# Bias of the third and fourth block by identity matmuls instead of vector adds, with a new written order

## The chip, the cores and the metric

The kernel runs on one core of a Trainium2 chip. A core has a matrix engine (TensorE, PE in the profile, with its weight loads listed apart as PEld), a vector engine (VectorE, DVE), a scalar engine for functions such as exp and ln (ScalarE, ACT), a general engine (GpSimd, POOL) and a queue engine that issues transfers (SyncE, SP). Each works through its own list of instructions in order, and waits are made with semaphores. Matmuls write to PSUM, eight banks of 512 f32 values in each of 128 partitions; everything else lives in SBUF. The metric is the time of one execution in microseconds (us); lower is better.

## The reference

Windowed attention with a linear distance bias and a few global keys, and after it a two-layer network with softplus, on every token:

```python
scores = scale * np.matmul(q, k.transpose(0, 1, 3, 2))      # B, H, S, D = 4, 8, 768, 64
rel = pos[:, None] - pos[None, :]
is_global = pos[None, :] < n_global                          # 8
is_local = (rel >= 0) & (rel < n_local)                      # 96
dist = np.where(is_global & ~is_local, float(n_local), np.abs(rel))
scores = scores + (-slopes[:, None, None] * dist)[None]
scores = np.where(is_global | is_local, scores, -1e9)
a = np.exp(scores - np.max(scores, axis=-1, keepdims=True))
a = a / (np.sum(a, axis=-1, keepdims=True) + 1e-09)
x = np.matmul(a, v)                                          # to 3072 tokens of 512
h = x @ w_in                                                 # 512 -> 2048
g = np.maximum(h, 0.0) + np.log1p(np.exp(-np.abs(h)))
return g @ w_out                                             # 2048 -> 512
```

## The kernel before, in words

A query block is 128 tokens of one sequence, and there are 24, numbered in the order of `UNITS` (L148): a unit is two neighbouring blocks whose q, k and v are loaded together. Blocks 0 and 1 are the first two of sequence 0, blocks 2 and 3 the first two of sequence 1. Two blocks make a group of 256 tokens for the network, 12 groups in all. With a window of 96, a block looks at its own 128 keys and, unless it is the first of its sequence, at those of the block before, into which the eight global keys are copied (`gk`, `gv`). A first block thus has 4 score tiles of 128 columns for each half of the heads (a "part"), any other has 8.

The steps of a block: q and k are cast to bf16 (`castq`, `castk`) and transposed, in units 0 to 2 by TensorE (`trq`, `trk`, L740, evacuated by `cpq`, `cpk`), from unit 3 on by transposing DMAs on the SP queue (L763, L770). The scores (`sc`, L875; L822 for block 0) go to PSUM, `s_ps[0]` and `s_ps[1]` of two banks each. The bias, a bf16 table that also holds the mask, is added in one of two ways. In `soften` (L887) VectorE adds it while it moves the scores from PSUM to an SBUF tile `z` (L901, steps `z`), and the exp on ScalarE (L908, steps `ex`) reads `z`. For blocks named in `PE_BIAS` (L157) the step `sb` (L856, and L812 for block 0) first multiplies the table by the identity matrix into the same PSUM columns, the score matmuls accumulate on it (`start=not biased`, L878), and the exp reads PSUM. No maximum is subtracted. Then come the products with v (`pv`, L927), which bring the sum of the weights in a 65th column, the division (`nm`, L938 and L939) and the transposition of the result into XT (`xt` by TensorE and `xc` in groups 0 to 2, later by DMA).

The network: `a{g}.{p}` is the first layer of group g, piece p of 8 (eight matmuls, L985, into `h_ps[p % 2]`), `e` and `ln` the softplus on ScalarE (L1000, L1011), `b` the second layer (L1032 in groups 0 and 1; from group 2 on seven products of a Strassen scheme, L519, with sums `ka` of the activations, L449, and `ws` of the weights, L414), `oe` and `oc` the evacuation and `st` the store (L557, L1064). The f32 weights arrive in eight pieces each (`win`, `wout`, L623) and are cast (`cin`, `cout`, L627). `a{g}.{p}` needs both pieces of its pair, so `a0.0` and `a0.1` need `cin0` and `cin1`, and `a0.6` and `a0.7` need `cin6` and `cin7`.

What runs where and in which order is written out in full in the string `ORDER` (L68 to L146): each word is a step and its engine (P PE, V DVE, A ACT, G POOL, S SP), and every engine works through its steps in that order. Nothing is scheduled at run time. 35 matmuls on zeros (`fill`, L1145) stand where TensorE has nothing to do in the first microseconds. Steps on SP are issued in order too, each after what it waits for; k and q of unit i are `ldk{i}.0`, `ldk{i}.1` and so on in units 0 to 2, single loads later.

Of the kernel before, what the change touches and what calls it, by code (L numbers as in the profile page):

```python
# [1300 lines left out]
```

## Time and profile before

| | |
|---|---|
| median of 3 runs | 212.99 us (211.81 to 213.7) |
| the profiled execution: time | 212.39 us |
| the profiled execution: span from first to last instruction | 210.6 us |
| mean granted TensorE clock | 0.999 |
| adds of the bias on DVE, 1024 columns (L901, biasA) | 38, mean 1216 ns |
| exp on ACT of 1024 columns from z (L908) | 38, mean 1051 ns |
| fillers on PE (L1145) | 35 |
| PE waiting for a k transposition by DMA | 1.3 us, once |
| moved by DMA | 40.98 MB |

A row of a timeline gives the start in us from the beginning of the span, how long it took, the engine and the line, the operation, what it writes and reads, and how many instructions are merged into it; in brackets stands the idle time of the engine before it and what ended that. A queue has a q behind its engine (SPq, ACTq). A matmul's record is longer than the time that it keeps PE, because matmuls overlap in the pipeline; the distance between two starts is the better measure.

### The profile page before, as it was taken

How to read it: one execution, taken by the hardware profiler on the slowest of the kernel's cores; microseconds unless marked ns; L12 is line 12 of the kernel's file. 1: busy time of each engine (PE TensorE's matmuls, PEld its weight loads, DVE VectorE, ACT ScalarE, POOL GpSimd, SP SyncE). 2: the span in 40 equal slices, each digit the busy share in tenths (PEclk: the TensorE clock that was granted, in tenths of full speed). 3: DMA queues.
4: the chain of work that ended last, by engine and by line, in shares of the span. 5: the costliest groups of instructions: out<-in, count | busy, mean ns of one | idle time of the engine just before them, and what ended most of it. 6: DMA issues, size and time to landing. Idle time of an engine off the chain costs nothing.

```text
span 210.6 us, 5494 instructions
## 1 busy us (share of the span) xinstructions
PE 201.3 (96%) x2211; PEld 164.4 (78%) x2211; DVE 156.1 (74%) x287; ACT 174.6 (83%) x248; POOL 105.5 (50%) x113
## 2 busy tenths in 40 slices
PE   5898899999999979999999999999999999999993
PEld 2465687655778868888988988888899889888883
DVE  5779699988788965889888878858883976023494
ACT  5768799998999998978789999896997999775710
POOL 4347668745954763455415783502126849129040
PEclk9999999999999999999999999999999999999999
DMA  5999999999999999999999599955641103400205
GB/s 196 337 355 386 387 357 363 336 209 242 221 304 191 221 214 271 240 166 288 209 170 225 180 181 272 146 124 128 153 99 28 25 5 102 150 0 0 103 0 199
DMA packets 70136, 40.98 MB, mean 195 GB/s; under 512 B 30432, under 2 KB 61664, under 8 KB 70112
## 3 DMA queue, kind: packets, MB, share of 16 engines
q1 hardware_dynamic: 69680, 39.99, 76.2%
q10 hardware_dynamic: 432, 0.66, 0.9%
q8 instruction: 17, 0.28, 0.6%
q14 instruction: 7, 0.06, 0.1%
HBM read 27.26 MB, written 6.29 MB: 159 GB/s over the span
## 4 chain that ended last, share of the span: by engine, by line
PE 68%; DMA 13%; POOL 5%; ACT 5%; DVE 4%; issue 2%; ACTq 0%; SPq 0%; POOLq 0%; DVEq 0%
PE h_ps L985 31%; PE o_ps L519 20%; DMA raw<-in_k_dram 5%; PE s_ps L875 4%; PE x_ps L927 4%; PE s_ps L1032 3%; DMA kT<-kb 3%; DMA raw<-in_q_dram 3%; DMA qT<-qb 2%; PE o_ps L1032 2%; POOL raw L449 2%; ACT pb L908 2%; ACT e L1000 2%; ACT g L1011 1%; POOL g L449 1%
## 5 line engine op out<-in xcount | busy, mean ns | idle before, releaser
L985 PE MATMUL h_ps<-XT,w_in_bf 128*128 128x256 bf16 x768 | 95.5, 273 | 1.5 <-POOL w_in_bf L627 1.3
L985 PEld LDWEIGHTS <-w_in_bf 128*128 128x128 bf16 x768 | 72.4, 98 | 13.1 <-POOL w_in_bf L627 1.9
L1000 ACT ACTIVATE e<-h_ps 128x512 f32<-128x512 f32 x96 | 60.2, 636 | 14.3 <-PE h_ps L985 13.9
L1011 ACT ACTIVATE g<-e 128x1024 bf16<-128x1024 f32 x48 | 50.0, 1057 | 0.4
L901 DVE TENSOR_TENSOR z<-s_ps,biasA 128x1024 f32<-128x1024 f32 x38 | 45.8, 1216 | 3.4 <-PE s_ps L875 2.0
L908 ACT ACTIVATE pb<-z 128x1024 bf16<-128x1024 f32 (+1 forms) x44 | 43.2, 992 | 1.1 <-DVE z L901 1.0
L519 PEld LDWEIGHTS <-g 128*128 128x128 bf16 x320 | 30.8, 98 | 3.6
L449 POOL TENSOR_TENSOR raw<-g 128x1024 bf16<-128x1024 bf16 x11 | 23.5, 2142 | 19.3 <-ACT g L1011 12.8
L677 POOL CAST vb<-raw 64x512 bf16<-64x512 f32 x31 | 20.4, 660 | 11.0 <-DMA raw<-in_v_dram 9.1
L449 POOL TENSOR_TENSOR g<-g 128x1024 bf16<-128x1024 bf16 x9 | 19.5, 2171 | 12.3 <-DVE raw L449 9.7
L793 POOL COPY vb<-vb 4x512 bf16<-4x512 bf16 x16 | 9.8, 612 | 31.7 <-PE x_ps L927 30.6
L519 PEld LDWEIGHTS <-raw 128*128 128x128 bf16 x240 | 23.1, 98 | 2.9
L519 PE MATMUL o_ps<-raw,raw 128*128 128x256 bf16 x192 | 24.1, 273 | 0.0
L519 PE MATMUL o_ps<-raw,g 128*128 128x256 bf16 x160 | 20.1, 273 | 0.0
L927 PEld LDWEIGHTS <-pb 128*128 128x128 bf16 x352 | 16.4, 98 | 4.3 <-ACT pb L908 0.9
L939 DVE TENSOR_TENSOR xs<-x_ps,rcp 128x256 bf16<-128x256 f32 x40 | 17.0, 424 | 1.4
L449 DVE TENSOR_TENSOR raw<-g 128x1024 bf16<-128x1024 bf16 x19 | 15.6, 827 | 2.7 <-ACT g L1011 2.7
L519 PE MATMUL o_ps<-w_out_bf,g 128*128 128x256 bf16 x128 | 16.1, 272 | 0.0
L927 PE MATMUL x_ps<-vb,pb 128*128 128x65 bf16 x304 | 15.8, 193 | 0.0
L938 DVE RECIPROCAL rcp<-x_ps 128x4 f32<-128x4 f32 x40 | 7.1, 179 | 10.3 <-PE x_ps L927 10.1
L1145 PE MATMUL x_ps<-blank 128*128 128x512 bf16 x35 | 12.2, 436 | 2.2 <-DVE blank L1084 2.2
L483 DVE TENSOR_TENSOR osb<-osb,o_ps 128x512 f32<-128x512 f32 x8 | 5.5, 686 | 10.3 <-PE o_ps L519 8.1
(109 smaller groups left out, 227.6 us busy)
## 6 DMA issues: line engine op xcount, KB each, us to landing
raw<-in_v_dram SPq DMA_DIRECT2D x12, 512.0 KB, 6.3
out_dram<-osb SPq DMA_DIRECT2D x22, 256.0 KB, 2.5
raw<-in_q_dram SPq DMA_DIRECT2D x9, 512.0 KB, 5.3
raw<-in_k_dram SPq DMA_DIRECT2D x9, 512.0 KB, 5.1
raw<-in_moe_w_in_dram SPq DMA_DIRECT2D x8, 512.0 KB, 9.3
raw<-in_moe_w_out_dram SPq DMA_DIRECT2D x8, 512.0 KB, 9.4
raw<-in_k_dram SPq DMA_DIRECT2D x6, 256.0 KB, 6.6
raw<-in_q_dram SPq DMA_DIRECT2D x4, 256.0 KB, 7.5
```

What stands on the lines that cost most here:

```text
L449: (nc.vector if eng == "DVE" else nc.gpsimd).tensor_tensor(dst, a[0], b[0], ALU.subtract)
L519: nc.tensor.matmul(psum(j), lhs[:, f // 2, f % 2, :], w(f), start=(f == 0 and not (chain and j in "267")), stop=(f == 7), skip_group_check ...
L677: copy_on[eng](dst, src)
L901: nc.vector.tensor_tensor(z, src, bias, ALU.add)
L908: nc.scalar.activation(pb[:, 0:nr, :].rearrange("p (y a) b -> p y (a b)", y=2), src, AF.Exp, scale=1.0 / root_d)
L927: nc.tensor.matmul(xv[:, h, :], pb[:, 4 * (h % 2) + 2 * part + h // 2 if lone else u_all * (2 * (h % 2) + h // 2) + u, :], vb_of(prev if u ...
L939: nc.vector.tensor_tensor(xs[:, 4 * part : 4 * part + 4, :], xv[:, :, 0:D], rcp[:][:, :, None].to_broadcast([P, 4, D]), ALU.mult,)
L985: last = nc.tensor.matmul(hv[:, j, :], w_in_bf[:, m, fb * P : fb * P + P], XT[g % NXG][:, m, :], start=(m == 0), stop=(m == NM - 1),)
L1000: nc.scalar.activation(e[:, p % 2, :, :].rearrange("p j (b t r) -> p (j b) r t", b=2, r=2), hb[:].rearrange("p (a r t) -> p a r t", a=4, r=2),
L1011: nc.scalar.activation(gt[:, 2 * p - 2 : 2 * p + 2, :].rearrange("p a t -> p (a t)"), e[:].rearrange("p a j t -> p (a j t)"), AF.Ln, bias=1.0,
L1032: nc.tensor.matmul(bank(key)[:, 0 : z - a], gt[:, fb, ns * P : ns * P + P], w_out_bf[:, fb, a:z], start=(fb == 0), stop=(fb == NFB - 1),)
L1145: nc.tensor.matmul(x_ps[:], blank[:, 0:P], blank[:])
```

## The change

`PE_BIAS` names blocks 2 and 3 as well. The four VectorE adds `z2.0`, `z2.1`, `z3.0` and `z3.1` are no longer made, and their exps read PSUM. Three steps come on TensorE: `sb2.0`, four identity matmuls of 256 columns, and `sb3.0` and `sb3.1`, two of 512 columns each. The string `ORDER` is another one throughout: steps stand elsewhere in their engine's list, and some casts, copies and sums of two operands have another engine. The loads of the first three units and of w_in are the same ones in another sequence. Everything else in the file is unchanged. Of `ORDER`, its beginning and the part around the transpositions of units 5 and 6 are shown:

```diff
 ORDER = """
-ldq0.1:A iota:G ldk0.1:S ldq0.0:A ldk0.0:S dl1a:V blank:V table:A ldq1.0:S dl1c:V fill0:P dl0a:V ldv0:S dl0b:V
-fill1:P dl0c:V ldq1.1:S fill2:P dl1e:V d0:G ident:G fill3:P ldk1.0:S biasTrue2:A d0e:V fill4:P ones:G fill5:P
-biasFalse2:V fill6:P biasFalse7:A biasFalse5:G biasFalse1:V castk0.1:A fill7:P biasFalse6:V biasTrue0:A fill8:P
-biasFalse3:A win0:S castk0.0:V biasTrue4:A fill9:P castq0.1:A castq0.0:V ldk1.1:S trk0.0:P biasTrue7:V castq1.0:A
-win1:S biasFalse0:V biasFalse4:A trq0.0:P ldv1:S cpk0.0:V fill10:P ldk2.0:S sb0.0:P cpq0.0:A biasTrue3:V fill11:P
-castv0.00:G win3:S cpk0.1:V cpq0.1:A fill12:P fill13:P biasTrue1:A fill14:P biasTrue6:G biasTrue5:V sc0.0:P fill15:P
-sb1.0:P castv0.11:G ex0.0:A win2:S castv0.01:V fill16:P ex0.1:A sc1.0:P castv0.10:G ldk2.1:S castq1.1:V sb1.1:P
-ex1.0:A pv0.0:P sc1.1:P nm0.0:V fill17:P ldq2.0:S ex1.1:A castk1.0:V pv0.1:P fill18:P castk1.1:V ldq2.1:S trq1.0:P
-nm0.1:V fill19:P trk1.0:P cpq1.1:V fill20:P cin1:G win5:S pv1.0:P cpk1.0:A cpq1.0:V pv1.1:P fill21:P cpk1.1:A
-fill22:P nm1.0:V xt0:P nm1.1:V sc2.0:P fill23:P castv1.11:A castv1.01:G win4:S fill24:P z2.1:V fill25:P xt1:P
-gv4.0:A castv1.10:G fill26:P win7:S z2.0:V fill27:P sc3.1:P xc1:A xc0:V cin0:G sc3.0:P ex2.0:A fill28:P z3.0:V
-ex2.1:A win6:S castv1.00:G a0.1:P cin3:A castk2.0:G z3.1:V wout0:S pv2.0:P a0.0:P cin2:G e0.1:A wout1:S fill29:P
-nm2.0:V a0.3:P e0.0:A castq2.0:G ldv2:S castk2.1:V ln0.0:A castq2.1:G wout3:S fill30:P pv2.1:P nm2.1:V gk4:G ex3.0:A
-trq2.0:P trk2.0:P cin5:G wout2:S cpq2.1:V xt2:P e0.3:A fill31:P a0.2:P cpk2.0:V xc2:A gv4.1:G wout4:S cin4:V
-fill32:P fill33:P e0.2:A pv3.0:P cpk2.1:V a0.5:P ex3.1:A cin7:G wout5:S nm3.0:V a0.4:P cpq2.0:V e0.5:A ln0.1:A
-pv3.1:P cin6:V sc4.0:P gv8.1:G nm3.1:V a0.7:P ldq3:S e0.4:A z4.0:V ln0.2:A cout0:G wout6:S xt3:P a0.6:P xc3:V e0.7:A
...
-z8.1:V xt7:S castv4.01:G a2.7:P e2.4:A castv4.11:V b1.1.12:P ex8.1:A ldq6:S ws3.1:V pv8.0:P a2.6:P st0.1.0:S ln2.2:A
-nm8.0:V trq5:S gk9:G b1.1.14:P castv4.10:V e2.6:A pv8.1:P sc9.0:P e2.7:A nm8.1:V gv9.1:G trk5.0:S castv5.00:A a3.0:P
-oc1.1.0:V castv5.11:G ln2.3:A ws3.7:G z9.0:V a3.1:P st1.1.0:S xt8:S e3.0:A b2.3:P ka2.7:V ex9.0:A a3.2:P gv9.0:V
-st0.0.0:S ka2.5:G z9.1:V e3.1:A ldv6:S b2.4:P ldk6:S e3.2:A ka2.1:V trk5.1:S ex9.1:A pv9.0:P a3.3:P castv5.10:G
-gk10:A a3.4:P ln3.0:A nm9.0:V ka2.6:V pv9.1:P e3.3:A sc10.0:P nm9.1:V gv10.0:G oe2.a:A a3.5:P e3.4:A z10.1:V ka2.2:G
-xt9:S b2.1:P e3.5:A ex10.1:A a3.6:P ldq7:S oe2.1:V ldv7:S gv10.1:G a3.7:P ln3.1:A z10.0:V gk11:G castv6.11:G b2.5:P
-e3.6:A castq6.0:V ex10.0:A castk6.0:G sc11.0:P trq6:S a4.0:P e3.7:A z11.0:V ln3.3:A castv5.01:G a4.1:P trk6.0:S
-castv6.01:G e4.0:A b2.2:P ex11.0:A trk6.1:S pv10.0:P a4.2:P oe2.c:V castq7.0:A nm10.0:V b2.7:P ldk7:S e4.1:A z11.1:V
-ldv8:S pv10.1:P ln3.2:A b2.6:P gv11.0:G nm10.1:V e4.2:A a4.3:P ka3.1:V ex11.1:A gv11.1:V a4.4:P oe2.7:V e4.3:A
-pv11.0:P ka3.7:V st2.1.0:S b3.3:P ln4.0:A xt10:S nm11.0:V ka3.5:G sc12.0:P ln4.1:A pv11.1:P b3.4:P z12.1:V trq7:S
...
+blank:V table:A ones:G ldk0.0:S ldq0.0:A iota:G fill0:P ldk0.1:S ldq0.1:A fill1:P ident:G dl1a:V fill2:P ldv0:S
+fill3:P ldq1.0:S dl0a:V dl0b:V fill4:P dl1c:V fill5:P dl0c:V dl1e:V fill6:P d0:G biasTrue1:A ldk1.0:S d0e:V fill7:P
+biasTrue0:A biasFalse1:V fill8:P castk0.0:G biasFalse2:A ldq1.1:S biasTrue7:V fill9:P biasFalse7:A fill10:P
+biasFalse6:A fill11:P biasTrue6:A ldk1.1:S castq0.0:V fill12:P fill13:P biasFalse5:V castk0.1:G win1:S biasTrue4:V
+castq0.1:A biasTrue3:A trk0.0:P ldv1:S biasFalse0:V biasTrue5:V biasFalse4:A trq0.0:P biasTrue2:A cpk0.1:V
+biasFalse3:A fill14:P fill15:P cpq0.1:A fill16:P cpk0.0:V fill17:P win0:S cpq0.0:A sb0.0:P castv0.01:V castv0.10:G
+sc0.0:P castv0.11:V fill18:P sb1.0:P ex0.0:A castv0.00:G sc1.0:P ex0.1:A castq1.0:V sb1.1:P ex1.0:A sc1.1:P ldq2.1:S
+castk1.0:V pv0.0:P fill19:P win2:S castk1.1:G fill20:P nm0.0:V ex1.1:A fill21:P win3:S fill22:P castq1.1:G ldk2.0:S
+trq1.0:P ldk2.1:S pv0.1:P trk1.0:P cpq1.0:A ldq2.0:S nm0.1:V pv1.1:P fill23:P cpk1.0:A cpq1.1:V pv1.0:P fill24:P
+cpk1.1:A castv1.00:G win4:S xt0:P nm1.0:V fill25:P cin1:G sb2.0:P xc0:V sc2.0:P nm1.1:V win5:S castv1.01:G fill26:P
+cin0:V fill27:P ex2.0:A xt1:P win7:S fill28:P gv4.1:G castv1.10:A fill29:P sb3.0:P xc1:V ex2.1:A sc3.0:P castq2.1:G
+pv2.0:P a0.0:P gv4.0:A win6:S nm2.0:V castv1.11:G ex3.0:A fill30:P pv2.1:P cin2:G a0.1:P wout0:S e0.0:A nm2.1:V
+wout1:S castk2.0:V sb3.1:P cin3:G e0.1:A wout3:S fill31:P sc3.1:P fill32:P xt2:P castk2.1:G ex3.1:A a0.2:P xc2:V
+castq2.0:G ln0.0:A pv3.0:P cin4:V ldv2:S a0.3:P nm3.0:V e0.2:A trk2.0:P gk4:V e0.3:A pv3.1:P cin5:V trq2.0:P
+cpk2.1:A nm3.1:V a0.5:P cpq2.0:A cpk2.0:V cin7:G ln0.1:A a0.4:P cpq2.1:V wout2:S e0.5:A xt3:P cin6:V sc4.0:P e0.4:A
+wout6:S ln0.2:A gk8:V a0.7:P z4.1:V ws0.6:G a0.6:P e0.7:A xc3:V ex4.1:A fill33:P cout1:V fill34:P a1.1:P ldq3:S
...
+b1.1.14:P ex8.0:A st0.0.0:S a2.7:P ldq6:S ws3.4:V castv4.00:G a2.6:P trk5.1:S ex8.1:A castv4.01:V e2.7:A oc1.1.0:V
+pv8.0:P gk9:G st1.0.0:S castq5.0:G e2.6:A sc9.0:P nm8.0:V ln2.2:A a3.1:P z9.1:V ws3.3:G trq5:S ln2.3:A a3.0:P z9.0:V
+castv4.11:G pv8.1:P trk5.0:S b2.3:P e3.0:A gv9.0:G e3.1:A nm8.1:V a3.2:P castv4.10:G ex9.0:A ka2.7:V ldk6:S gv9.1:G
+a3.3:P xt8:S e3.2:A ka2.6:V ex9.1:A b2.4:P castv5.00:G ka2.1:V ldv6:S pv9.0:P e3.3:A a3.4:P castv5.01:G gk10:A
+oe2.a:A nm9.0:V a3.5:P ln3.1:A castq6.0:V pv9.1:P ka2.5:V e3.4:A sc10.0:P ldv7:S gv10.0:G nm9.1:V ln3.0:A b2.1:P
+gv10.1:G z10.1:V xt9:S e3.5:A a3.6:P ka2.2:G oe2.1:V ex10.1:A a3.7:P ldq7:S z10.0:V e3.6:A b2.5:P gk11:A e3.7:A
+castv6.00:V trq6:S castk6.0:G sc11.0:P ex10.0:A b2.2:P z11.0:V castv6.11:G ln3.2:A st1.1.0:S pv10.0:P trk6.0:S
+a4.0:P castv6.01:G nm10.0:V castv7.10:G a4.1:P oe2.c:V e4.0:A trk6.1:S castv5.11:G z11.1:V pv10.1:P a4.2:P e4.1:A
+gv11.1:G ldv8:S ex11.0:A gv11.0:V castv7.01:G b2.7:P castv6.10:V ln3.3:A b2.6:P nm10.1:V e4.2:A castq7.0:V a4.3:P
+ln4.0:A oe2.7:V a4.4:P ka3.7:V ex11.1:A sc12.0:P ka3.1:V ka3.5:G ldq8:S pv11.0:P e4.3:A b3.3:P z12.0:V xt10:S
...
 BIASA_ON = ["ACT"]
-PE_BIAS = (0, 1)
+PE_BIAS = (0, 1, 2, 3)
 PE_KEYS = {
```

More of the change, by code (lines that the diff above doesn't have):

```diff
@@ new lines @@
+sc6.0:P oc1.0.0:A nm5.1:V castv3.01:A gv6.1:G ldk5:S z6.0:V xt5:P castv3.00:G b1.1.0:P xc5:A b1.1.2:P gv6.0:G z6.1:V
+b1.1.4:P ex6.0:A a2.1:P castk4.0:G trq4:S ex6.1:A pv6.0:P a2.0:P ws2.7:G nm6.0:V gk7:A e2.1:A trk4.0:S pv6.1:P
+sc7.0:P e2.0:A nm6.1:V castv5.10:G a2.3:P ln2.0:A z7.0:V gv7.0:G ldq5:S a2.2:P gv7.1:G trk4.1:S z7.1:V ex7.0:A
+castv3.10:G b1.1.6:P b1.1.8:P ldv4:S ws1.6:V ex7.1:A pv7.0:P b1.1.10:P nm7.0:V st0.1.0:S ws3.1:G sc8.0:P e2.3:A
+pv7.1:P xt6:S e2.2:A a2.5:P nm7.1:V ln2.1:A ws3.7:G z8.0:V a2.4:P xt7:S e2.5:A castk5.0:G b1.1.12:P z8.1:V e2.4:A
@@ new lines @@
+ln4.1:A nm11.0:V b3.4:P z12.1:V ldk7:S pv11.1:P a4.5:P oe3.a:A nm11.1:V ka3.6:G ex12.1:A sc13.0:P xt11:S e4.4:A
+b3.1:P ex12.0:A z13.0:V e4.5:A pv12.0:P trq7:S a4.6:P castq8.0:G nm12.0:V ex13.0:A a4.7:P oe3.1:V ldk8:S e4.6:A
+ka3.2:V pv12.1:P b3.5:P castk7.0:G e4.7:A z13.1:V castv7.00:A st2.1.0:S b3.2:P ln4.2:A trk7.1:S nm12.1:V a5.1:P
+oe3.c:V ln4.3:A a5.0:P xt12:S ex13.1:A b3.7:P e5.0:A trk7.0:S gk14:G pv13.0:P b3.6:P ka4.1:V e5.1:A nm13.0:V
+castk8.0:A a5.2:P st2.0.0:S oe3.7:V pv13.1:P a5.3:P e5.2:A st3.1.0:S nm13.1:V trq8:S gv14.1:A castv8.10:V b4.3:P
```

90 lines of the change are left out of this document (40 added, 50 removed).

## The prediction

> **What bounds the kernel now.** I read the page first: the busy shares, then the slices.
>
> ```profile
> span 210.6 us, 5494 instructions
> PE 201.3 (96%) x2211; PEld 164.4 (78%) x2211; DVE 156.1 (74%) x287; ACT 174.6 (83%) x248; POOL 105.5 (50%) x113
> DMA  5999999999999999999999599955641103400205
> GB/s 196 337 355 386 387 357 363 336 209 242 221 304 191 221 214 271 240 166 288 209 170 225 180 181 272 146 124 128 153 99 28 25 5 102 150 0 0 103 0 199
> ```
>
> A PE busy for 96% says little by itself, because fillers count as busy too. So next comes the view by stages (busy us of PE, PEld, DVE, ACT, POOL, then clock, DMA share, GB/s):
>
> ```profile
> 18.70:29.00 10.30, 9.28 (x114) 7.61 (x115) 8.19 (x17) 8.66 (x13) 6.56 (x10) 1.00 1.06 381
> 29.00:76.00 47.00, 46.86 (x497) 34.61 (x496) 41.73 (x69) 45.28 (x63) 31.99 (x38) 1.00 1.10 269
> 76.00:79.00 3.00, 1.73 (x16) 1.30 (x14) 1.63 (x2) 2.97 (x5) 1.34 (x4) 1.00 1.50 133
> 79.00:207.00 128.00, 127.86 (x1438) 112.55 (x1439) 90.10 (x161) 104.96 (x147) 57.02 (x45) 1.00 0.60 138
> ```
>
> From 29 us to 207 us PE is idle for 0.14 + 1.27 + 0.14 us in all, and the 1.27 is one wait:
>
> ```profile
> 72.18 2.17 SPq L763 DMA_TRANSPOSE kT<-kb  x1
> 76.69 1.04 PE L519 MATMUL o_ps<-w_out_bf,g 128*128 128x256 bf16 x8
> 79.03 0.62 PE L875 MATMUL s_ps<-qT,kT 64*128 64x128 bf16 x16 [1.30 <-DMA kT<-kb]
> ```
>
> So the end is the moment at which the PE stream becomes dense, plus the PE work left then, plus the waits inside. Before 29 us the loads decide: DMA is full from the second slice on, and the last piece of w_in is cast here, after which a0.7, the last first-layer unit of group 0, can start:
>
> ```profile
> 28.01 0.69 DVE L627 CAST w_in_bf<-raw 128x1024 bf16<-128x1024 f32 x1
> 28.94 1.05 PE L985 MATMUL h_ps<-XT,w_in_bf 128*128 128x256 bf16 x8
> ```
>
> The cast ends at 28.70 and a0.7 starts at 28.94. All q, k, v of the first three units and all eight w_in pieces stand ahead of that cast in the SP queue of both kernels, only permuted, so this point is where to compare them.
>
> **The adds that go.** Four DVE instructions:
>
> ```profile
> 16.11 1.28 DVE L901 TENSOR_TENSOR z<-s_ps,bias 128x512 f32<-128x512 f32 x2
> 17.88 2.36 DVE L901 TENSOR_TENSOR z<-s_ps,biasA 128x1024 f32<-128x1024 f32 x2 [0.16 <-PE s_ps L875]
> 17.81 1.14 ACT L908 ACTIVATE pb<-z 128x512 bf16<-128x512 f32 x2
> 11.18 2.02 ACT L908 ACTIVATE pb<-s_ps 128x1024 bf16<-128x1024 f32 x2 [0.22 <-PE s_ps L875]
> ```
>
> That is 1.28 + 2.36 = 3.64 us of DVE. The exp stays: it reads s_ps instead of z, about 1.0 us for 1024 columns either way. All of this lies between 16 and 29 us, where loads are the limit, so I count the gain at nothing. The order spends it on casts: w_in pieces 0 and 5 go from POOL to DVE. If loads were not the limit, it would shorten the score-to-exp step by up to 1.2 us a tile.
>
> **The seeds that come.** Block 2 gets four of 256 columns, block 3 twice two of 512. The same things exist for blocks 0 and 1 (chain of waits: start, time on the chain, what):
>
> ```profile
> 8.21 0.44 PE h_ps L812 x4
> 10.16 0.43 PE s_ps L856 x2
> 10.59 0.22 PE x_ps L1145
> 10.81 0.35 PE s_ps L875 x8
> 23.36 1.07 PE s_ps L740 x16
> 24.43 0.22 PE o_ps L958 x4
> 24.87 0.87 PE h_ps L985 x8
> 26.17 0.24 PE o_ps L927 x8
> 28.45 0.55 PE s_ps L875 x16
> ```
>
> So 0.44 + 2 x 0.43 = 1.30 us more PE work. All of it stands ahead of a0.7. What has to hide it is the slack of PE before 28.94; if there is none, the price is the whole 1.30.
>
> **Does PE still reach a0.7 in time?** The path of block 0 and 1 in the kernel before:
>
> ```profile
> 0.72 1.56 ACTq L582 DMA_DIRECT2D raw<-in_q_dram  x2
> 2.31 1.28 ACT L341 ACT_TABLE_LOAD   x1 [2.31 <-issue]
> 6.81 0.43 DVE L645 CAST qb<-raw 128x512 bf16<-128x512 f32 x1 [1.27 <-DMA raw<-in_q_dram]
> 7.01 0.62 ACT L645 CAST qb<-raw 128x512 bf16<-128x512 f32 x1 [0.72 <-DMA raw<-in_q_dram]
> 9.44 0.40 PE L822 MATMUL h_ps<-qT,kTa 64*128 64x128 bf16 x8
> 15.44 0.40 PE L875 MATMUL s_ps<-qT,kTa 64*128 64x128 bf16 x8
> 15.76 0.42 DVE L939 TENSOR_TENSOR xs<-h_ps,rcp 128x256 bf16<-128x256 f32 x1
> 18.69 1.05 PE L985 MATMUL h_ps<-XT,w_in_bf 128*128 128x256 bf16 x8 [0.53 <-POOL w_in_bf L627]
> ```
>
> Call T the start of block 0's scores, 9.44 here. Two things move it in the new order. The half of q that lands last is cast by ACT (0.62) and no longer by DVE (0.43): +0.19. And on ACT the table load now stands ahead of the two q loads, where before it stood behind them. Bounds: nothing, if the load is issued while the table still loads, and 1.28 us, the table row, if it waits. No row shows a DMA issue behind a running ACT instruction; the only row with both has them the other way round. I take 0.3 as T's shift, nearer to nothing, because the DMA engines have k to move meanwhile, and keep 0.2 to 1.5.
>
> [...]
>
> From T, block 2's scores were T + 6.0, after the last k evacuation. Now a seed of 0.44 stands between, but the next thing, the transposition of block 1's xs, has to wait for block 1's norm anyway: it ended at 16.18, T + 6.74, and the new order puts one 0.41 us copy of XT ahead of it, so T + 7.15. Then 0.22 + two fillers 0.44 + seed 0.43 + block 3's first scores 0.35 + half a pv 0.12: a0.0 at about T + 8.7. From a0.0 to a0.7 the new order has six first-layer units (6 x 0.87), three fillers (0.66), pv 0.12 + 2 x 0.24, seed 0.43, scores 0.35 + 0.55, two xs transpositions 0.44, the two of unit 2 1.07: 9.3 us. So PE could be at a0.7 at T + 18.0 = 27.4 + 0.3 = 27.7 us without waits, 28.9 at the far bound. The cast of the last w_in piece was done at 28.70. The seeds are thus hidden, with about 1 us to spare. Of the work behind a0.7, xs transposition 3 (0.22) has moved ahead of it and one more filler (0.22) behind it: nothing in sum. I put +0.1 for this whole stretch, between -0.2 and +0.8.
>
> **The order after 29 us.** DVE, ACT and POOL trade casts and small copies; PE is dense and none of it is waited for today. What PE did wait for is a k transposition on the SP queue. In the kernel before, unit 5's second one stands behind v6 and k6 loads; in the new one it goes ahead of unit 5's q, so these 1.3 us should go. What is late next: unit 5's first k transposition now has that one and a store ahead of it, and block 12's scores stand 1.1 us sooner in PE's order behind the same bytes.
>
> ```profile
> 67.20 1.19 SPq L763 DMA_TRANSPOSE kT<-kb  x1
> 68.50 0.52 SPq L1064 DMA_DIRECT2D out_dram<-osb  x1
> kT<-kb SPq DMA_TRANSPOSE x14, 3.8
> 72.63 0.62 PE L875 MATMUL s_ps<-qT,kT 64*128 64x128 bf16 x16
> ```
>
> Issued at 67.20 and 3.8 later (the median of all), about 71.0, against scores at 72.63: 1.6 us of lead. One more transposition and one more store ahead cost SP 1.19 + 0.52 = 1.7, and by the sums of PE's order the scores of block 10 stand 0.8 us later than before, so 0.7 is left; block 12 loses 1.1 of its own. These two places run with a microsecond of lead or less. A load of 512 KB ahead costs 512 KB over 269 GB/s, the rate from 29 to 76 us, 1.95 us. Ends: both hold (sum -1.3) or both are late by a load (-1.3 + 3.9 = +2.6). I take 0.65 for each, a third of a load, since the queue has the same loads ahead of them as before: -1.3 + 1.3 = 0.
>
> **Sum.** The profiled execution took 212.39 us for a span of 210.6, and the median of the three times is 212.99, so I carry the difference over to it: 0 (adds) + 0 (seeds) + 0.1 (start) + 0 (transpositions) gives 213.1 us.
>
> **The rivals.** First, transpositions late, ending slower: at blocks 10 and 12 the k or q transposition lands after PE gets there, by a full load each. For it: DMA is full in that stretch (share 1.10), SP issues strictly in order, and the leads are short by the sum above. Against: no load has been moved ahead of them. Price +2.6 + 0.1: 215.7, and past 1% as soon as the landing is more than 1.7 us behind PE at both (2 x 1.7 - 1.3 = 2.1). Other transpositions of the new order could fail likewise. Chance 0.40.
>
> Second, the wait goes and nothing replaces it, while the early loads run at the full rate. The second and third slices moved 337 and 355 GB/s where the fifth moved 387: (50 + 32) / 387 of a 5.27 us slice, 1.1 us, that another order of issue might save; PE could use it, as 27.7 is 1.2 below 28.94. Then -1.3 - 1.1: 210.6. Against: both slowdowns would have to vanish together. Chance 0.18.
>
> Third, the seeds are not hidden: q late by 1.3 and other waits eat the spare microsecond, so 1.30 us of PE work shows on top of 212.99: 214.3. Chance 0.10.
>
> My forecast has 0.32. That the change doesn't do what it says I leave out: the four adds are gone from DVE's list and the eight new seeds stand in PE's.
>
> **Numbers.** Within 1% (2.1 us, about what a measurement of this kernel tells from no change) lie the forecast and the third rival: 0.42. Slower by more: 0.40, the first. Faster by more: 0.18, the second. The range leaves about a tenth out on each side: from 210.9, which cuts half of the second rival, to 216.6, a microsecond above the first, for another place of its kind. The likeliest case's own range is 211.8 (waits gone) to 214.2 (start at its far bound).
>
> **What would show it.** In the profile after: no L901 on the s_ps of blocks 2 and 3, sixteen seed matmuls at L812 and L856 instead of eight; T near 9.7 and a0.7 near 28.8 confirm the start, T near 11 the table load's cost; PE dense from 29 us; no wait at block 11's scores, and at blocks 10 and 12 waits of some tenths (forecast), of 2 us each (first rival), or none (second). Wrong would be a wait on another engine than SP's transpositions past 29 us, or a PE stream that becomes dense a microsecond away from 28.9.

## The result, and the profile after

Each kernel ran 22 times. The kernel before took 212.77 us at the median (211.02 to 215.57), the changed one 213.52 us (212.54 to 215.78). The ratio is 1.005, 95% interval 1.0026 to 1.0074: slower, by less than the 1% that was called no change. The prediction said 213.1 us. The mean granted clock of the single executions matters for the experiments below: 17 of the changed kernel's 22 had 0.997 or more and took 212.5 to 214.3 us, five had 0.992 and took 214.5 to 215.8 us.

The profiled execution of the changed kernel has a span of 211.2 us against 210.6. Its stages, in the view that was shown of before (busy us of PE, PEld, DVE, ACT, POOL, then clock, DMA share, GB/s):

```profile
span 211.2 us, 5492 instructions
PE 203.2 (96%) x2219; PEld 164.8 (78%) x2219; DVE 154.3 (73%) x279; ACT 173.4 (82%) x247; POOL 106.4 (50%) x118
18.70:29.00 10.30, 9.51 (x123) 7.69 (x121) 7.07 (x17) 8.58 (x13) 4.97 (x7) 1.00 1.05 387
29.00:76.00 47.00, 45.33 (x480) 33.27 (x479) 39.61 (x64) 43.78 (x62) 31.48 (x38) 1.00 1.12 265
76.00:79.00 3.00, 3.00 (x37) 2.54 (x37) 2.95 (x4) 2.80 (x6) 2.98 (x2) 1.00 1.13 212
79.00:207.00 128.00, 127.25 (x1428) 111.48 (x1422) 91.63 (x159) 105.42 (x144) 57.29 (x52) 1.00 0.64 136
```

PE has eight instructions more, the new seeds, and DVE eight fewer, four of which are the adds; the other four, in sum, are steps that changed engine. The hole between 76 and 79 us is closed (3.00 of 3.00 busy, before 1.73). Two new ones are open: 1.67 us of idle time between 29 and 76 us, and 0.75 us behind 79 us, where before there was 0.14 each. The rows at the start and at the old and new holes, from the timelines of the engines (start, us, engine, line):

```profile
0.73 1.28 ACT L341 ACT_TABLE_LOAD   x1 [0.73 <-PEq L1282]
0.76 1.54 ACTq L582 DMA_DIRECT2D raw<-in_q_dram  x2
6.13 0.62 ACT L645 CAST qb<-raw 128x512 bf16<-128x512 f32 x1 [1.17 <-DMA raw<-in_q_dram]
8.88 0.40 PE L822 MATMUL h_ps<-qT,kTa 64*128 64x128 bf16 x8
27.74 0.69 DVE L627 CAST w_in_bf<-raw 128x1024 bf16<-128x1024 f32 x1 [0.34 <-DMA raw<-in_moe_w_in_dram]
28.49 1.92 PE L985 MATMUL h_ps<-XT,w_in_bf 128*128 128x256 bf16 x16 [0.22 <-DVE w_in_bf L627]
64.53 0.40 PE L927 MATMUL x_ps<-vb,pb 128*128 128x65 bf16 x8 [0.26 <-POOL vb L677]
66.68 1.92 PE L985 MATMUL h_ps<-XT,w_in_bf 128*128 128x256 bf16 x16 [1.20 <-DMA XT<-xs]
74.51 0.62 PE L875 MATMUL s_ps<-qT,kT 64*128 64x128 bf16 x16
78.66 0.62 PE L875 MATMUL s_ps<-qT,kT 64*128 64x128 bf16 x16
86.85 0.40 PE L875 MATMUL s_ps<-qT,kTa 64*128 64x128 bf16 x8
167.42 2.13 POOL L449 TENSOR_TENSOR g<-g 128x1024 bf16<-128x1024 bf16 x1
167.47 2.37 DVE L677 CAST vb<-raw 64x512 bf16<-64x512 f32 x1
169.87 0.18 DVE L938 RECIPROCAL rcp<-x_ps 128x4 f32<-128x4 f32 x1
170.57 0.40 PE L927 MATMUL x_ps<-vb,pb 128*128 128x65 bf16 x8 [0.33 <-DVE xs L939]
174.17 0.40 PE L927 MATMUL x_ps<-vb,pb 128*128 128x65 bf16 x8 [0.23 <-DVE xs L939]
```

Rows 74.51, 78.66 and 86.85 are the scores of blocks 10, 11 and 12: no bracket, so PE waits at none of them. Instead it waits for the cast of block 8's v (row 64.53) and for XT of group 3 (66.68), and near 170 us for a division that VectorE could not begin before 169.87, because a cast of 64 x 512 values (castv11.11) kept it for 2.37 us.

Added up over PE's whole list, where each distance from one step's start to the next is set against the usual distance of such a step: a0.7 comes 0.45 us earlier; from 70 to 80 us PE loses 0.23 us where it lost 1.60 (-1.37); from 60 to 70 us 1.80 in place of 0.30 (+1.50); from 160 to 180 us 1.38 in place of 0.31 (+1.07); all other stretches together -0.17. The sum is +0.58, and PE's last step begins at 206.96 in place of 206.37.

### The profile page after: what moved, and what is told of

Its sections match the earlier page's. It is cut to its first block, busy times and chain, and to the rows that moved or that the text cites. A ratio compares the mean times of both kernels' runs of the same rounds, so it can differ in the third digit from the quotient of the medians.

```text
span 211.2 us, 5492 instructions
## 1 busy us (share of the span) xinstructions
PE 203.2 (96%) x2219; PEld 164.8 (78%) x2219; DVE 154.3 (73%) x279; ACT 173.4 (82%) x247; POOL 106.4 (50%) x118
## 4 chain that ended last, share of the span: by engine, by line
PE 77%; DMA 14%; DVE 5%; issue 2%; SPq 1%; POOL 1%; DVEq 0%; POOLq 0%
PE h_ps L985 35%; PE o_ps L519 24%; DMA raw<-in_moe_w_in_dram 8%; PE x_ps L927 4%; PE s_ps L875 4%; PE s_ps L1032 3%; DMA raw<-in_v_dram 3%; PE o_ps L1032 3%; DMA XT<-xs 3%; PE x_ps L519 2%; DVE z L901 1%; PE s_ps L519 1%; SPq L582 1%; POOL vb L677 1%; DVE xs L939 1%
## 5 line engine op out<-in xcount | busy, mean ns | idle before, releaser
L1000 ACT ACTIVATE e<-h_ps 128x512 f32<-128x512 f32 x96 | 59.0, 633 | 12.6 <-PE h_ps L985 12.0
L901 DVE TENSOR_TENSOR z<-s_ps,biasA 128x1024 f32<-128x1024 f32 x36 | 43.0, 1216 | 3.6 <-PE s_ps L875 2.6
L908 ACT ACTIVATE pb<-z 128x1024 bf16<-128x1024 f32 (+1 forms) x40 | 40.0, 1008 | 3.2 <-DVE z L901 2.7
L449 POOL TENSOR_TENSOR g<-g 128x1024 bf16<-128x1024 bf16 x10 | 21.8, 2177 | 21.4 <-DVE raw L449 16.2
L677 POOL CAST vb<-raw 64x512 bf16<-64x512 f32 x29 | 19.9, 687 | 15.5 <-DMA raw<-in_v_dram 10.7
L449 POOL TENSOR_TENSOR raw<-g 128x1024 bf16<-128x1024 bf16 x8 | 17.0, 2130 | 15.2 <-ACT g L1011 13.6
L449 DVE TENSOR_TENSOR raw<-g 128x1024 bf16<-128x1024 bf16 x22 | 16.1, 749 | 6.8 <-ACT g L1011 3.3
L927 PEld LDWEIGHTS <-pb 128*128 128x128 bf16 x352 | 16.5, 97 | 4.7 <-issue 1.9
L793 POOL COPY vb<-vb 4x512 bf16<-4x512 bf16 x20 | 12.5, 626 | 12.0 <-PE x_ps L927 8.6
L927 PE MATMUL x_ps<-vb,pb 128*128 128x65 bf16 x304 | 15.8, 193 | 0.8 <-DVE xs L939 0.6
L875 PE MATMUL s_ps<-qT,kT 64*128 64x128 bf16 x224 | 9.9, 218 | 0.0
```

The lines of the kernel that those rows point to most:

```text
L449: (nc.vector if eng == "DVE" else nc.gpsimd).tensor_tensor(dst, a[0], b[0], ALU.subtract)
L677: copy_on[eng](dst, src)
L875: nc.tensor.matmul(reg if unit_of(n) in WIDE else reg.rearrange("p (r t) -> p r t", r=2), kt[rows, 2 * part + m, :], qv(rows, 2 * part + m ...
L901: nc.vector.tensor_tensor(z, src, bias, ALU.add)
L908: nc.scalar.activation(pb[:, 0:nr, :].rearrange("p (y a) b -> p y (a b)", y=2), src, AF.Exp, scale=1.0 / root_d)
L927: nc.tensor.matmul(xv[:, h, :], pb[:, 4 * (h % 2) + 2 * part + h // 2 if lone else u_all * (2 * (h % 2) + h // 2) + u, :], vb_of(prev if u ...
```

## The experiments

All twelve, with the median of the kernel before in the same comparison, the ratio with its interval, and what the profiled execution shows:

| kernel | median us (before) | ratio (95%) | span, granted clock |
|---|---|---|---|
| seeds, old order | 215.77 (212.74) | 1.018 (1.013 to 1.023) | 213.5, 1.000 |
| adds, new order | 214.91 (212.74) | 1.007 (1.003 to 1.012) | 213.3, 0.992 |
| no bias on blocks 2, 3 | 214.60 (212.74) | 1.010 (1.006 to 1.015) | 211.8, 1.000 |
| seeds twice | 214.45 (212.74) | 1.010 (1.006 to 1.013) | 214.0, 0.990 |
| v of unit 5 later | 215.53 (212.79) | 1.013 (1.009 to 1.017) | 213.6, 0.992 |
| new start, old rest | 217.03 (212.79) | 1.019 (1.013 to 1.026) | 212.3, 1.000 |
| old order, transposition earlier | 214.27 (212.79) | 1.007 (1.003 to 1.010) | 213.2, 0.992 |
| changed kernel again | 214.05 (212.79) | 1.008 (1.005 to 1.012) | 212.3, 1.000 |
| v of unit 4 first | 213.02 (213.12) | 1.000 (0.996 to 1.004) | 211.2, 0.999 |
| castv11.11 on ScalarE | 212.26 (213.12) | 1.001 (0.996 to 1.006) | 210.1, 1.000 |
| ka8.2 on VectorE | 212.44 (213.12) | 0.999 (0.995 to 1.003) | 213.2, 0.992 |
| four steps placed anew | 211.32 (212.55) | 0.993 (0.990 to 0.996) | 209.4, 1.000 |

Line numbers of most of these kernels are one less than those of the changed kernel (L926 for L927), since their order has one text line less.

### Is it the seeds or the order?

Four kernels take the two halves of the change apart. The first has the seeds in the order of before; the four adds are gone, and the exps of blocks 2 and 3 are moved forward on ACT:

```diff
-PE_BIAS = (0, 1)
+PE_BIAS = (0, 1, 2, 3)
-sc2.0:P ... z2.1:V ... z2.0:V ... sc3.1:P ... sc3.0:P ex2.0:A ... z3.0:V ex2.1:A ... z3.1:V ... ex3.0:A ... ex3.1:A
+sb2.0:P sc2.0:P ... ex2.0:A ex2.1:A sb3.1:P sc3.1:P ... sb3.0:P sc3.0:P ... ex3.0:A ex3.1:A
```

> The seeds alone, in the old order: the four adds go, the seeds stand ahead of their scores, and four exps of blocks 2 and 3 are moved forward on ACT, since they now free PSUM. Theory (loads set the start of a0.7, PE has room ahead of it, and the new order brings the loss by its own waits): no change against the kernel before, ratio 0.998 to 1.002, with the 1.3 us wait for a k transposition near 77 us still there. Rival (the 1.30 us of seeds are paid in full and the new order gave half of it back): ratio 1.006.

It came out at 1.018. PE waits of that kernel (what waited, for what, total us, times, longest), and the rows from its timeline:

```profile
PE s_ps L874 <- DMA kT<-kb: 2.4, 3, 1.6
PE s_ps L739 <- ACT pb L907: 1.6, 2, 1.3
18.06 0.59 PE L855 MATMUL s_ps<-biasA,ident 128*128 128x512 bf16 x2 [0.48 <-ACT pb L907]
24.78 0.61 PE L739 MATMUL s_ps<-ident,qb 128*128 128x128 bf16 x8 [1.30 <-ACT pb L907]
30.76 1.05 PE L984 MATMUL h_ps<-XT,w_in_bf 128*128 128x256 bf16 x8
```

The seed `sb3.1`, the first of block 3 to be issued here, and the transpositions of unit 2 wait for ACT's exp: it is now the exp that empties the banks of `s_ps`, where before a VectorE add did, and in the old order ACT comes to it later. a0.7 starts at 30.76, 1.82 us later than before. The sum closes: between 15 us and a0.7 PE waits 0.48 + 1.30 + 0.31 = 2.09 us for ACT, and the seeds are 1.30 us of work by the prediction's sum, but the waits of 0.53, 0.73 and 0.29 us that the kernel before has there (1.55 us, most of it for w_in) are gone; 2.09 + 1.30 - 1.55 = 1.84. So the seeds' work alone would have fitted into the old waits. The price comes from the PSUM banks that the seeds and the scores keep until ACT has read them. (The exps' places on ACT are part of this edit, so the 1.8 us belong to both.) The k transpositions cost 2.4 us in place of 1.3, which together with the 1.82 makes up the 2.9 us by which the span is longer. Both expectations missed this.

The other three have the new order, with the adds back, with no bias at all on blocks 2 and 3 (their scores are then unmasked), and with every seed of these blocks issued twice:

```diff
-PE_BIAS = (0, 1, 2, 3)
+PE_BIAS = (0, 1)
-sb2.0:P ... sc2.0:P nm1.1:V ... sb3.0:P ... sc3.0:P ... sb3.1:P ... sc3.1:P
+sc2.0:P nm1.1:V z2.0:V z2.1:V ... sc3.0:P z3.0:V ... sc3.1:P z3.1:V
```

> The new order alone: seeds taken out, the four adds put back on VectorE behind their scores. Theory: as the changed kernel, ratio 1.002 to 1.006, with the waits of the new order (about 1.2 us for an XT transposition near 66 us, about 1.2 us in all between 169 and 173 us) still there. Rival (seeds paid): 1.3 us less than the changed kernel, ratio 0.997 to 0.999.

```diff
-        if biased:
+        if biased and n < 2:
-start=not biased, stop=True, skip_group_check=biased,
+start=not biased or n >= 2, stop=True, skip_group_check=biased and n < 2,
```

> The changed kernel without the eight new seeds and without adds: blocks 2 and 3 get no bias. Theory: the seeds are hidden, so 0 to 0.3 us less than the changed kernel, ratio 1.002 to 1.005, a0.7 within 0.3 us of 28.5. Rival (seeds paid): 1.3 us less, ratio 0.997 to 0.999, a0.7 near 27.2.

```diff
-            for part in parts:
+            for part in parts * (2 if n >= 2 else 1):
```

> The changed kernel with each of the new seeds issued twice (the second overwrites the first): 1.30 us more PE work ahead of a0.7. Theory: PE lost 0.73 us behind unit 2's k transposition and 0.29 us ahead of a0.7, so about 1.0 us of it is hidden, and a0.7 comes 0.3 to 0.6 us later: ratio 1.004 to 1.007. Rival (no room): 1.3 us later, ratio 1.010 to 1.011.

a0.7 starts at 28.28 with the adds, at 28.18 with no bias, at 28.23 with the seeds doubled and at 28.49 in the changed kernel:

```profile
28.28 1.92 PE L984 MATMUL h_ps<-XT,w_in_bf 128*128 128x256 bf16 x16
28.18 1.92 PE L984 MATMUL h_ps<-XT,w_in_bf 128*128 128x256 bf16 x16 [0.25 <-DVE w_in_bf L626]
28.23 1.92 PE L985 MATMUL h_ps<-XT,w_in_bf 128*128 128x256 bf16 x16
```

No seeds and twice the seeds differ by 0.05 us: in the new order the seeds are hidden behind the loads, and the changed kernel's 28.49 is the landing of its last w_in piece (row 27.74 above). Nor do the times go with the amount of seeds: all four kernels of the new order, the changed one among them, lie 0.5% to 1% above the kernel before. In the changed kernel the new order costs the time, not the bias. The expectations of these three had this cause right and were too low in size: 1.002 to 1.006, 1.002 to 1.005 and 1.004 to 1.007 stood against 1.007, 1.010 and 1.010. The last is the number of its rival, but not by the rival's way, for which a0.7 had to come 1.3 us later.

### Where the new order loses it

The changed kernel once more:

> The changed kernel once more, beside the others on the same chip: ratio 1.003 to 1.008 as before. If its waits past 60 us depend on when transfers happen to land, the places of the waits differ in this profile from the first one; if they are set by the order alone, the same steps wait by the same amounts within 0.3 us.

Its profile waits at the same steps, XT at 66.8 us and the cast of v at 64.7 us, with a cast of 2.37 us near 168 us again, and at one new step, a4.0 (0.6 us). So most of the places are set by the order. The sizes differ by up to 0.3 us, and that the landing of the transfers makes this difference is likely but not shown. The next two try the obvious repair and the half of the new order that had gained:

```diff
-oc0.0.0:A ldv5:S nm5.0:V
+oc0.0.0:A nm5.0:V
-nm6.1:V castv5.10:G a2.3:P
+nm6.1:V a2.3:P
-a2.4:P xt7:S e2.5:A
+a2.4:P xt7:S ldv5:S e2.5:A
-a3.4:P castv5.01:G gk10:A
+a3.4:P castv5.01:G castv5.10:G gk10:A
```

> The changed kernel with the load of v of unit 5 moved behind the second XT transposition of group 3 on SP, and the cast that reads it moved too. Theory: in the changed kernel the first layer's 1.2 us wait for XT (a3.1 at 66.68) and the 0.3 us wait of block 8's product with v come from SP's queue, in which a load that is needed some 10 us later goes first; both go, PE waits less than 0.4 us in all between 60 and 70 us, and the ratio to the kernel before falls from 1.005 by 1.5 of 212.8 to 0.998 (0.996 to 1.001). Rival: the transfers are late by the load on the DMA engines and not by their place; then waits of 1 us or more stay between 60 and 80 us and the ratio is 1.003 to 1.010.

> The changed kernel's order up to and with a1.1 (seeds of blocks 2 and 3 in it), and from there on the order of the kernel before. Theory: the new start is worth the 0.7 us by which a1.1 came earlier (31.35 to 30.68), and what the changed kernel loses is lost by its later order; so block 11's scores still wait some 1.3 us for a transposition, nothing else does, and the ratio is 0.997 (0.995 to 0.999). Rival: the transfers of the old rest come at their own time, so that the 0.7 us are waited away by 80 us (a wait at block 11's scores of 2.0 us): ratio 1.000 (0.999 to 1.002). If the seeds themselves cost time, 1.003 or more.

Both missed. With v of unit 5 later, XT is no longer waited for, but block 8's product with v now waits 2.46 us for a cast on VectorE. The same happens in the kernel with the adds in the new order, from which the rows below are (PE, then VectorE and GpSimd):

```profile
66.43 0.60 PE L926 MATMUL x_ps<-vb,pb 128*128 128x65 bf16 x8 [2.45 <-DVE vb L676]
63.19 3.09 DVE L676 CAST vb<-raw 64x512 bf16<-64x512 f32 x1
62.73 0.90 POOL L676 CAST vb<-raw 64x512 bf16<-64x512 f32 x1 [0.80 <-DMA raw<-in_v_dram]
63.58 0.20 POOL L782 COPY kT<-kTa 128x32 bf16<-128x32 bf16 x1
63.73 1.03 POOL L644 CAST qb<-raw 128x1024 bf16<-128x1024 f32 x1
64.74 1.26 POOL L413 TENSOR_TENSOR raw<-raw,raw 128x512 bf16<-128x512 f32 x1
```

The cast (castv4.01) begins while GpSimd is at work. GpSimd's fourth instruction in a row ends at 66.00, and the cast ends 0.28 us after that. In the changed kernel's own profile the same cast happened to begin 0.02 us ahead of GpSimd's (63.59 against 63.61), and took 0.42 us; near 168 us a cast that began 0.05 us behind GpSimd's sum took 2.37 us. Hundredths of a microsecond decide this step of the new order.

In the kernel with the new start and the old rest, the old rest pays at two places: PE waits 1.08 us at 32.39 for a cast of w_out, and at block 11's scores 1.80 us for the transposition that had cost 1.30, near the 2.0 us that its rival gave; the ratio of 1.019 is beyond the rival's too.

```profile
32.39 0.59 PE L1031 MATMUL s_ps<-w_out_bf,g 128*128 128x512 bf16 x2 [1.08 <-POOL w_out_bf L626]
80.44 0.62 PE L874 MATMUL s_ps<-qT,kT 64*128 64x128 bf16 x16 [1.80 <-DMA kT<-kb]
```

a1.1 had come 1.08 us earlier than before (30.27 against 31.35), but 0.43 of this is a product of the second layer that stands ahead of a1.1 in the kernel before and behind it here; block 11's scores come 1.41 us later (80.44 against 79.03). The seeds are not what cost it: a0.7 starts at 28.08, 0.86 us earlier than before. This profile is of its fastest execution, 214.4 us; what the others lost beyond that, up to 220 us, no profile shows, and it stays open. The edit that the prediction priced at -1.3 was then made alone in the kernel before:

```diff
-e3.1:A ldv6:S b2.4:P ldk6:S e3.2:A ka2.1:V trk5.1:S ex9.1:A
+e3.1:A trk5.1:S ldv6:S b2.4:P ldk6:S e3.2:A ka2.1:V ex9.1:A
```

> The kernel before with one step moved: the second k transposition of unit 5 goes ahead of the load of v of unit 6 on SP. Theory: the wait of 1.3 us at block 11's scores goes and nothing takes its place, which is what the prediction assumed as the best case of that edit: ratio 0.994 (0.992 to 0.996). Rival: the next transposition, product with v or XT is late by about as much; ratio 0.998 to 1.002, with a wait of 0.5 us or more on another transfer between 70 and 90 us.

```profile
76.24 1.03 PE L518 MATMUL o_ps<-raw,raw 128*128 128x256 bf16 x8 [2.41 <-ACT osb L479]
75.60 0.58 ACT L479 COPY osb<-o_ps 128x512 f32<-128x512 f32 x1 [3.23 <-DMA out_dram<-osb]
```

Block 11's wait went. Instead ACT waited 3.23 us for a store to free its `osb`, PE 2.41 us for ACT, and the kernel got slower, 1.007: the rival's kind of loss at a larger price. (The profile is of one of the four executions, of 12, whose mean clock is 0.992.) The store stood directly ahead of the transposition; it landed 4.6 us after its issue (70.97 to 75.52), in the kernel before 2.5 us (70.36 to 72.89). That the transposition behind it is what held it is not shown, and two stores speak against it: one with a transposition of XT directly behind it took 2.7 us in the kernel before (68.50 to 71.19) and one 2.8 us in this one (69.11 to 71.91; the median of its 22 stores is 2.7 us).

### What a long wait costs

In five of the profiled executions PE waits once for 2.4 us or more. The windows of the kernel with seeds twice (waits 2.52 us up to 66.44, here for a late load of v) and of the old order with the transposition earlier (2.41 us up to 76.24); the column after POOL is the granted clock:

```profile
64.00:66.00 2.00, 0.00 (x0) 0.00 (x0) 0.47 (x2) 2.00 (x4) 0.47 (x1) 1.00 0.88 32
66.00:68.00 2.00, 1.56 (x25) 1.36 (x26) 1.25 (x3) 0.76 (x1) 2.00 (x4) 0.62 1.16 340
68.00:70.00 2.00, 2.00 (x11) 1.43 (x12) 1.89 (x2) 0.00 (x0) 1.36 (x2) 0.52 1.18 314
70.00:74.00 4.00, 4.00 (x45) 3.62 (x43) 3.35 (x6) 3.17 (x5) 2.76 (x4) 1.00 1.14 205
```

```profile
76.00:78.00 2.00, 1.76 (x13) 1.47 (x13) 0.64 (x2) 2.00 (x4) 0.00 (x0) 0.81 1.19 291
78.00:80.00 2.00, 2.00 (x12) 1.39 (x10) 1.79 (x3) 2.00 (x4) 0.82 (x2) 0.50 1.23 286
80.00:82.00 2.00, 2.00 (x27) 1.48 (x25) 0.07 (x1) 1.88 (x3) 1.94 (x3) 0.84 1.18 288
```

Behind the wait the clock is at half for some 3.4 us: (1 - 0.62) x 2 + (1 - 0.52) x 2 = 1.7 us of TensorE time lost in the first, (0.19 + 0.50 + 0.16) x 2 = 1.7 us in the second. The same stretch shows in all five (adds in the new order, seeds twice, v of unit 5 later, transposition earlier, ka8.2 on VectorE), and in none of the nine other profiles, whose longest wait past 20 us is 1.8 us. The half clock doesn't always begin where the wait ends: with v of unit 5 later the wait ends at 66.33, the clock is 1.00 from there to 67.83, and 0.50 from 67.83 to 71.25 (in windows: 0.96 from 66 to 68 us, 0.50 from 68 to 70, 0.84 from 70 to 74). A wait of 2.5 us therefore costs about 4.2, an estimate from these windows; the step distances used above give 3.9 us for the wait of 2.45 us in the kernel with the adds in the new order. 1.7 us is 0.8% of the span, which is why the mean clock of these executions is 0.990 to 0.992. That a shorter wait leaves the clock alone was seen only up to 1.8 us.

By the mean clock of the single executions (0.992 or less), such a wait occurred in 7 of 34 executions of the changed kernel and in 5 of 6 with v of unit 5 later, but also in 7 of 92 of the kernel before in the experiments' comparisons. It explains a part of the spread only: single executions with a clock of 1.000 reached 215.2 us (changed kernel) and 216.35 us (kernel before).

### The cast beside GpSimd, and the repair

Two kernels take castv11.11 and GpSimd's sum apart in opposite ways:

```diff
-trk11.1:S castv11.10:A sc22.0:P ... gk23:G castv11.11:V ka8.2:G
+trk11.1:S castv11.10:A castv11.11:A sc22.0:P ... gk23:G ka8.2:G
```

> The changed kernel with one cast of v of unit 11 (castv11.11) on ScalarE and not on VectorE. Theory: on VectorE it took 2.37 us because GpSimd ran a sum of 2.13 us at the same time; on ScalarE it takes some 0.6 us, the division of block 22 comes 1.8 us earlier, and the 1.2 us that TensorE lost in three places between 169 and 174 us go: ratio 1.000 (0.997 to 1.004), the waits at 60 to 70 us as before. Rival: something else holds block 22 (its exps, its sums on VectorE); less than 0.4 us of the 1.2 comes back, ratio 1.004 to 1.009.

```diff
-gk23:G castv11.11:V ka8.2:G b8.1:P
+gk23:G castv11.11:V ka8.2:V b8.1:P
```

> The changed kernel with the sum ka8.2 on VectorE behind castv11.11 and not on GpSimd beside it. If GpSimd's sum is what stretches VectorE's cast, castv11.11 takes 0.4 to 0.7 us in place of 2.37 and the sum some 0.8 us behind it, so that the division of block 22 comes about 1 us earlier. If the cast is slow for its own operands (64 partitions of f32 from a late load), it stays at 2.2 us or more and the division is later than before.

VectorE of the second kernel, and PE of the first:

```profile
170.76 0.43 DVE L676 CAST vb<-raw 64x512 bf16<-64x512 f32 x1
171.22 0.69 DVE L448 TENSOR_TENSOR g<-g 128x1024 bf16<-128x1024 bf16 x1
171.83 0.18 DVE L937 RECIPROCAL rcp<-x_ps 128x4 f32<-128x4 f32 x1
```

```profile
167.57 0.41 PE L926 MATMUL x_ps<-vb,pb 128*128 128x65 bf16 x8
170.22 0.41 PE L926 MATMUL x_ps<-vb,pb 128*128 128x65 bf16 x8
173.08 0.41 PE L926 MATMUL x_ps<-vb,pb 128*128 128x65 bf16 x8
```

Without GpSimd's sum beside it the same cast takes 0.43 us, and VectorE does the sum as well in 0.69 us, both together in half the time that the cast took beside GpSimd's sum. With the cast on ScalarE, PE goes from 167.57 to 173.08 through the steps that took from 167.42 to 174.17: 5.51 us in place of 6.75, and the 1.24 us come back. That GpSimd's sum stretches the cast, and that the stretched cast costs TensorE 1.2 us, is shown from both sides by these profiles. The ratios of 1.001 and 0.999 fit this, but their intervals are wide: the first reaches to 1.006 and doesn't exclude the changed kernel's 1.005. (The second kernel's profile has a span of 213.2 us because its product with v of block 8 waited 2.74 us for a late load.)

For the hole near 65 us the first attempt moved v of unit 4 itself to the front:

```diff
-b1.0.14:P ws2.6:V castv3.11:G ... castv5.10:G ... castv3.10:G b1.1.6:P b1.1.8:P ldv4:S
+b1.0.14:P ws2.6:V ldv4:S castv3.11:G ... castv4.00:G ... castv3.10:G castv4.01:G b1.1.6:P b1.1.8:P
-xt7:S e2.5:A ... castv4.00:G ... castv4.01:V ... castv5.01:G ... castv11.11:V
+xt7:S ldv5:S e2.5:A ... castv5.01:G castv5.10:G ... castv11.11:A
```

> The changed kernel with the load of v of unit 4 some 8 us earlier on SP, that of unit 5 behind the second XT transposition of group 3, block 8's first cast of v in the place of one of unit 5's, its second cast (castv4.01) on GpSimd and not on VectorE, and castv11.11 on ScalarE. Theory: the new order loses its time at two places, the product with v of block 8 (0.4 to 2.6 us, and where it is 2.5 us TensorE's clock is down for some 3 us behind it) and the two late results of block 22 near 170 us; both come from a cast of v, and both go. PE waits less than 0.5 us between 60 and 70 us, the granted clock is 0.997 or more in every profile, nothing of 0.3 us is lost between 168 and 175 us; span 209.5 (209.0 to 210.2), ratio 0.993 (0.990 to 0.997). Rival: the waits come from a full DMA and move on; another transfer is waited for by 1 us or more before 90 us, ratio 1.000 or more.

Its rival came true. The hole at 65 us shrank to a wait of 0.31 us for ScalarE; castv4.00 then waited for its load, the cast of unit 3 behind it on GpSimd came late, and PE waited 0.84 us at block 7's product with v and 1.45 us at a4.0 for XT. Ratio 1.000. The last kernel left that load where it was:

```diff
-oc0.0.0:A ldv5:S nm5.0:V ... nm6.1:V castv5.10:G a2.3:P
+oc0.0.0:A nm5.0:V ... nm6.1:V a2.3:P
-xt7:S e2.5:A ... castv4.00:G ... castv4.01:V ... castv5.01:G gk10:A
+xt7:S ldv5:S e2.5:A ... castv4.00:G castv4.01:G ... castv5.01:G castv5.10:G gk10:A
-sc10.0:P ldv7:S gv10.0:G ... xt9:S e3.5:A ... castv11.10:A ... castv11.11:V
+sc10.0:P gv10.0:G ... xt9:S ldv7:S e3.5:A ... castv11.10:A castv11.11:A
```

> The changed kernel with four steps placed anew: castv11.11 on ScalarE; castv4.01 on GpSimd behind castv4.00, so that no cast of block 8's v meets GpSimd on VectorE; the load of v of unit 5 behind the second XT transposition of group 3, with the cast that reads it; and the load of v of unit 7 behind the second XT transposition of group 4. Theory: the waits at block 8's product with v (0.4 us in the run with castv11.11 alone) and at a3.1 (1.3 us) go, and with them the longer ones that take the clock down; a4.0 waits 0.8 us or less for XT. Span 208.8 (208.2 to 209.8) against 210.1 of that run, ratio to the kernel before 0.992 (0.988 to 0.997), clock 0.997 or more. Rival: the load of v of unit 5 or 7 is now late for its cast, GpSimd waits for it, and a product with v of block 9 to 14 waits by 1 us or more; ratio 1.000 or more.

```profile
span 209.4 us, 5494 instructions
PE h_ps L984 <- DMA XT<-xs: 0.5, 1, 0.5
PE x_ps L926 <- POOL vb L676: 0.4, 1, 0.4
PE s_ps L874 <- DMA kTa<-kb: 0.4, 1, 0.4
```

It took 211.32 us, 0.993 (0.990 to 0.996) of the kernel before, as expected, and it is faster than both kernels of this case. What each of the four steps gives, and whether the seeds gain anything in this order, was not tried. Its longest wait past 29 us is 0.5 us, and all 12 of its executions had a clock of 0.999 or more and lay within 210.2 to 212.6 us.

## Why the prediction was right in its number, and where not

**What bounds the start: right for the changed kernel.** There a0.7 waits for the last cast of w_in (27.74 + 0.69 = 28.43, a0.7 at 28.49). In the kernel before it didn't quite: the cast had ended at 28.70, and a0.7 followed block 4's scores, the last row of the prediction's chain, at 28.94. The +0.1 was mis-sized: a0.7 came 0.45 us earlier. 0.27 of this is the cast (28.01 to 27.74), whose piece landed sooner, with 387 GB/s in place of 381 in that stretch; the other 0.18 is that PE is no longer behind the cast. The first is the second rival's mechanism, with a quarter of its 1.1 us.

**Adds at nothing: right in this order.** With the adds back in the new order a0.7 starts 0.2 us earlier (28.28). The reason given was incomplete: the adds also empty PSUM, and in the old order going without them costs 1.8 us, the moved exps included.

**Seeds hidden: right.** None, once or twice gives 28.18, 28.49 and 28.23. The spare microsecond was there too: with the seeds doubled, a0.7 no longer waits for the cast (no bracket in row 28.23). The third rival (0.10) is out.

**T: wrong sign, small.** Predicted +0.3, measured 8.88 - 9.44 = -0.56. The 0.3 was the author's choice between two bounds. The far bound is out: the table loaded from 0.73 on for 1.28 us, and the q loads left at 0.76, 0.03 us behind its start and not behind its end (2.01). The late half of q was there earlier than before (its cast began at 6.13, before at 6.81 and 7.01). As the loads bound a0.7, none of it showed.

**The 1.3 us wait at block 11 goes: right** (row 78.66).

**What is late next: the step that failed.** The prediction looked for it among the k transpositions, and gave blocks 10 and 12 0.65 us each. They wait for nothing. What PE paid in this profile, +1.50 near 65 us and +1.07 near 170 us, comes from three other things: the load of v of unit 4 in SP's queue behind that of unit 5, which is needed some 15 us later; the transposition of XT behind both; and a cast of v on VectorE beside GpSimd. Two of these the prediction could have read from the new order, by asking for each load on SP what stands ahead of it and when that is needed. The third it dismissed in the sentence "DVE, ACT and POOL trade casts and small copies; PE is dense and none of it is waited for today". By its own test ("wrong would be a wait on another engine than SP's transpositions past 29 us") it was wrong there. That the number held is in part luck. For what is late next, +1.3 was put in, and it cost 1.50 + 1.07 = 2.57, twice as much. The start made up for 0.55 of this (-0.45 in place of +0.1), the rest of PE's list for 0.17, and the old wait for 0.07, so that the sum is +0.58 in place of +0.1.

**The first rival** (0.40, a price of 2.6 us) had the right kind and not the place: where a transfer or a cast is late by 2.5 us, PE pays about 4.2 us with the clock counted in, and five executions with the lower clock took 214.5 to 215.8 us, near its 215.7. That they had such a wait is concluded from their clock; no profile of them was kept. In most executions the wait stays short.

## What to carry to other kernels

When an order is rewritten, price the moved loads and casts as well as the edit that gives the change its name: for each, what now stands ahead of it on its queue, and what runs on the engine beside it. A stall that is removed in a dense stream gives its time back only as far as the steps behind it are ready that much earlier: the edit that removed a wait of 1.3 us was followed, in the old order, by one of 2.4 us elsewhere. A wait on TensorE can cost more than its length: one of 2.5 us cost about 4.
